# Turning half of the attention keys on VectorE: clustered attention and a gated long convolution on one Trainium2 core

## The chip, the cores and the metric

The kernel runs on one core of one Trainium2 chip. A core has five engines with a queue each: TensorE (PE in the profile, PEld for its weight loads), VectorE (DVE), ScalarE (ACT), GpSimd (POOL) and SyncE (SP), which here only issues DMA transfers. They wait for each other by semaphores. The metric is the device time of one execution in microseconds, the median of several runs.

## What is computed

Two layers follow each other. The first is attention in which a query sees only the keys of its own cluster; the cluster is the centroid with the largest cosine. The second multiplies three projections of the result, the second of them convolved over the sequence by way of a Fourier transform, and projects the product.

```python
# batch 4, heads 8, sequence 768, head size 64, 16 centroids per head
q_assign = argmax(einsum('bhsd,hcd->bhsc', q_n, c_n))      # q_n, k_n, c_n: rows of length 1
k_assign = argmax(einsum('bhsd,hcd->bhsc', k_n, c_n))
mask   = q_assign[:, :, :, None] == k_assign[:, :, None, :]
scores = where(mask, q @ k.T / 8, -1e9)
attn   = softmax(scores);  o = attn @ v
x = o.transpose(0, 2, 1, 3).reshape(B, S, 512)
x1, x2, x3 = split(x @ w_proj, 3)
x2_conv = irfft(rfft(x2, axis=1) * rfft(filter_fft, axis=0), axis=1)
out = (x1 * x2_conv * x3) @ w_out
```

The order in which the keys of a head are taken does not matter, as long as V stands in the same order.

## The kernel before

The 32 heads are worked through in eight groups `n` of four heads, and a group in two pairs `pr` of two heads. `build` makes a list of operations, each with the engines that may run it and a duration for each (`op(("PE", 1.42), ...)`), a due time, and what it reads and writes. `Plan.place` then lays them out in time: at each step the engine that can start first takes, of the operations ready for it, the one that is due first. `NUDGE` adds a number to the due time of each operation by its place in the list, `ONLY` binds some operations to one of their engines. The result is a fixed order for each engine's queue; on the chip the engines only follow it and wait for each other.

**Loads.** `load_qk` (L313 on) brings the Q and the K of a pair, two transfers each, into one of four buffers `qkraw`: partition `p` gets the rows `6p` to `6p+5` of both heads, so each transfer has 768 runs of 64 numbers (256 bytes). `load_v` (L326) brings V into one of three buffers `vraw` in one transfer, in the same row order.

**Routing** (`routing`, L572 on). Scores need Q and K with the head dimension on the partitions. For groups 2 to 7 `tr2` (L592 to L594) turns Q and K of a pair by twelve 128x128 transposes on TensorE into three PSUM banks, and three copies of 512 columns (L597) on ScalarE or VectorE bring them to `qkP`. Groups 0 and 1 do it in blocks of three transposes (`tr`, L607) with one copy of 384 columns each. Casts to bf16 (L613) make the operands `augs` of the scores. `sim` (L627) compares Q and K with the centroids; on VectorE two transposes in 32x32 blocks (L632), a maximum (L638), a comparison (L640) and one more transpose (L642, `lock=True`) give the cluster of each row; `hits` (L653, L655) and eight small transfers (`masks`, L497) add the mask rows to `augs`.

**Attention** (`attention`). For each of the six key tiles `sk` of a pair: three score blocks of 512 columns on TensorE (L84 by way of `columns`, or L82 at full width), three exponentials on ScalarE into a buffer `p` of five (L694, L697), the product with V on TensorE (`pv`, L708: eight matmuls, at least 1.29 us in the profile), and the running sum of the `p` tiles in `acc` for the softmax's denominator. The first two tiles are added in three parts on VectorE or GpSimd (L725), the others one by one on VectorE (L729). Then `acc` is summed over partitions by transfers that accumulate (L762) or by a matmul (L742), and the reciprocal goes over DRAM (L766 to L779) to `rb`, which scales the output into `xT` (L808).

**The second layer** (`hyena`) of a batch of eight heads fills the gaps of the next two groups: projections (L843 and `G`), the transform as matmuls, products on VectorE (L857 to L959), the output projection and the store. That of the last batch forms the tail.

An operation marked `lock` on GpSimd is made to wait for the last such operation of VectorE ahead of it in the plan.

Of the kernel before, what the change touches and what calls it, by code (L numbers as in the profile page):

```python
# [19 lines left out]
Alu = mybir.AluOpType  # L20
PSUM = bass.MemoryType.PSUM

B, H, S, D, NC = 4, 8, 768, 64, 16
# [9 lines left out]
NV = 3  # L33
NU = 4
ROWS = 16
LEAD = 0.0
# [228 lines left out]
def build(T):  # L265
# [27 lines left out]

    def T_(name, i):
        return lambda: getattr(T, name)[i]
# [10 lines left out]
    def alu(e):  # L306
        return T.nc.vector if e == "DVE" else T.nc.gpsimd
# [7 lines left out]
    def load_qk(n, pr, j, due, after=()):  # L315
        s = qslot[n, pr, j] = len(loads) % NQK
        loads.append(1)

        src = lambda: (T.q, T.k)[j][n // 2, 4 * (n % 2) + 2 * pr:4 * (n % 2) + 2 * pr + 2].rearrange("h (p t) d -> p t h d", t=NT)
        for x in range(2):  # L320
            for half in ((0,), (1,)) if n == pr == 0 else ((0, 1),):
                t = slice(3 * half[0], 3 * half[-1] + 3)
                op({"SP": .66, "ACT": .66} if n == 0 else ("SP", .66), lambda e, x=x, t=t: dma(e)(
                    T.qkraw[s][:, t, x], src()[:, t, x]), due, w=[("qkraw", s, x, c) for c in half],
                   byts=98e3 * len(half), kind="load", after=after, lat=.3 if n else -.5)

    def load_v(n, pr, due, after=()):
        op(("SP", .6), lambda e: T.nc.sync.dma_start(
            T.vraw[(2 * n + pr) % NV], T.v[n // 2, 4 * (n % 2) + 2 * pr:4 * (n % 2) + 2 * pr + 2].rearrange(
                "h (p t) d -> p h (t d)", t=NT)), due, w=[("vraw", (2 * n + pr) % NV)], byts=LOAD, kind="load",  # L330
           after=after)
# [242 lines left out]
    def routing(n):  # L574
# [5 lines left out]
        for u in range(8):  # L580
            z, ch = u // 2, u % 2
            pr, j = z // 2, z % 2
            due = beg + (u - (.9 * (u % 4) if n > 1 else 0)) * (end - 22 - beg) / 8 if n else 3 + u
            if n == 0 and u == 4:
                got = first_masks(0)
            s = qslot[n, pr, j]
            raw = lambda s, i: T.qkraw[s][:, i].rearrange("p h d -> p (h d)")
            if n > 1 and z % 2 == 0 and ch == 0:
                h = Bank(cls, 3)
                ss = [qslot[n, pr, x] for x in range(2)]  # L590

                def tr2(e, ss=ss, h=h):  # L592
                    for i in range(2 * NT):
                        T.nc.tensor.transpose(bank(h.ids[i // 4])[:, ts(i % 4, 128)], raw(ss[i // NT], i % NT), T.ident[:, ::-1] if 3 <= i < NT else T.ident)  # L594
                op(("PE", 1.42), tr2, due, r=[("qkraw", s, x, c) for s in ss for x in range(2) for c in range(2)] + ["ident"], w=[h], alloc=h)
                for c in range(3):
                    op(EV512, lambda e, pr=pr, c=c, h=h: copy(e, T.qkP[pr][:, ts(c, 512)], bank(h.ids[c])), due + 1.6,  # L597
                       r=[h], w=[("qkT", 2 * pr + x, y) for x, y in ((0, 0), (0, 1), (0, 2), (1, 0), (1, 1), (1, 2))[2 * c:2 * c + 2]],
                       free=[h])
            elif n < 2:  # L600
                h = Bank(cls)

                def tr(e, s=s, ch=ch, j=j, h=h):
                    if n == 0:
                        awake(h)
                    for t in range(3):
                        T.nc.tensor.transpose(ap(h)[:, ts(t, 128)], raw(s, 3 * ch + t), T.ident[:, ::-1] if ch > j else T.ident)  # L607
                op(("PE", .36 if n else .58), tr, due, r=[("qkraw", s, x, c) for x in range(2) for c in ((0, 1) if n else (ch,))] + ["ident"] + ["cold"] * (n == 0), w=[h], alloc=h)
# [22 lines left out]
        for ch in range(2):  # L631
            op(("DVE", .57), lambda e, ch=ch, h=h: V().transpose(T.sim[:, ch], bank(h.ids[ch])[:, :384]), b0 + 1.4 + .1 * ch,  # L632
               r=[h], w=[("sim", ch, 0), ("sim", ch, 1)], free=[h])
# [8 lines left out]
        op(("DVE", .98), lambda e: V().transpose(T.ohB[:], words().rearrange("p m c -> p (m c)")), b0 + 4, r=both("oh"),  # L642
           w=["ohB"], lock=True)
# [640 lines left out]
```

## Time and profile before

| | |
|---|---|
| median of three runs | 369.32 us (369.24 to 369.35) |
| profiled execution | 369.39 us |
| its span, first to last instruction | 367.7 us |
| granted clock of TensorE | 0.999 |
| transposes L594 on TensorE | 144, weight loads 15.6 us |
| copies of qkP on VectorE | 5 of 512 columns, 3.3 us; 8 of 384 columns, 4.3 us |
| DMA packets | 90,405, of which 78,248 under 512 bytes |
| transfers issued by SP | 240 |

Times in the rows of groups are: busy time in all and mean of one in ns, then the idle time of the engine just ahead of such instructions and what ended it. Matmuls overlap each other in the pipeline, so the sum of their means is more than their busy time. A line of a helper, such as L84 or L282 and L284 (`copy` on ScalarE and on the other engines), stands for all who call it; the names of the tiles tell them apart.

### The profile page before, as it was taken

To read this page: it belongs to the slowest core of one execution; us is meant where nothing else is said; L and a number is where in the kernel's file an instruction comes from. 1 tells how busy PE (TensorE), PEld (TensorE's weight loads), DVE (VectorE), ACT (ScalarE), POOL (GpSimd) and SP (SyncE) were. 2 spreads that over 40 slices of the span, in tenths; PEclk is the share of its full clock that TensorE was granted. 3 is DMA by queue.
4 is the path that set the end of the run, shared out by engine and by line. 5 is a ranking of instruction groups with operands and counts; after the bars stand their busy time and mean duration, and the time that the engine had idled before them with its cause. 6 is when DMAs were issued, how large, how long until landed. Compare 5 with 4: busy or idle time off the path is not lost.

```text
span 367.7 us, 8671 instructions
## 1 busy us (share of the span) xinstructions
PE 357.7 (97%) x3322; PEld 207.4 (56%) x3322; DVE 342.5 (93%) x479; ACT 265.0 (72%) x496; POOL 119.3 (32%) x160
## 2 busy tenths in 40 slices
PE   8899999999999999999999999999999999999985
PEld 4455554556555655655555665566554655566662
DVE  7999999997999899999999999999998999999993
ACT  7999978877986867878679756798574768434242
POOL 7734131312043824322520033351220424016610
PEclk9999999999999999999999999999999999999999
DMA  7977994555655929487658947646486650110124
GB/s 177 247 140 170 191 220 101 146 127 142 174 109 71 178 40 208 80 182 90 109 66 193 260 111 173 118 92 71 88 120 162 152 77 2 47 45 2 57 118 171
DMA packets 90405, 46.20 MB, mean 126 GB/s; under 512 B 78248, under 2 KB 84092, under 8 KB 90364
## 3 DMA queue, kind: packets, MB, share of 16 engines
q1 hardware_dynamic: 85884, 36.25, 41.0%
q0 software_dynamic: 2752, 8.98, 17.7%
q10 hardware_dynamic: 1728, 0.43, 0.5%
q8 instruction: 26, 0.43, 0.5%
q14 instruction: 15, 0.12, 0.1%
HBM read 31.59 MB, written 7.40 MB: 106 GB/s over the span
## 4 chain that ended last, share of the span: by engine, by line
PE 88%; DVE 4%; ACT 3%; issue 2%; DMA 1%; ACTq 0%; POOL 0%; DVEq 0%; POOLq 0%
PE bank L84 38%; PE pair L708 32%; PE bank L843 6%; PE bank L594 4%; PE bank L627 3%; PE bank L742 1%; PE bank L607 1%; DMA qkraw<-in_k_dram 1%; DVE acc L729 1%; PE bank L475 1%; ACT p L697 1%; DVE qkP L284 1%; ACT qkP L282 1%; ACT aug L282 0%; PE bank L799 0%
## 5 line engine op out<-in xcount | busy, mean ns | idle before, releaser
L708 PE MATMUL pair<-p,vraw 128*64 128x385 f32 x768 | 142.6, 488 | 0.0
L697 ACT ACTIVATE p<-bank 128x512 f32<-128x512 f32 x192 | 108.2, 610 | 24.1 <-PE bank L84 20.0
L729 DVE TENSOR_TENSOR acc<-p,acc 128x1536 f32<-128x1536 f32 x64 | 111.8, 1747 | 2.8 <-POOL aug L284 0.8
L84 PE MATMUL bank<-aug,aug 80*64 80x512 bf16 (+3 forms) x744 | 83.8, 326 | 1.4 <-ACT p L697 0.7
L708 PEld LDWEIGHTS pair<-p,vraw 128*64 128x64 f32 x768 | 55.4, 136 | 44.3 <-issue 37.4
L84 PEld LDWEIGHTS <-aug 80*64 80x64 bf16 (+1 forms) x744 | 45.7, 109 | 41.7 <-issue 27.1
L694 ACT ACTIVATE p<-bank 128x512 f32<-128x512 f32 x96 | 57.8, 608 | 15.2 <-PE bank L84 13.0
L762 POOL DMA_DIRECT2D acc<-acc x30 | 23.7, 801 | 84.1 <-DMA acc<-acc 34.6
L284 POOL CAST aug<-qkP 64x768 bf16<-64x768 f32 x29 | 26.8, 931 | 66.4 <-DVE acc L729 43.9
L84 PE MATMUL bank<-xT,wpj 128*64 128x384 bf16 x504 | 47.8, 326 | 0.3 <-ACT p L697 0.2
L84 PEld LDWEIGHTS <-wpj 128*64 128x64 bf16 x504 | 30.3, 110 | 14.6 <-issue 3.4
L282 ACT COPY qkP<-bank 128x512 f32<-128x512 f32 (+1 forms) x47 | 24.0, 561 | 15.0 <-PE bank L594 8.1
L725 POOL TENSOR_TENSOR acc<-p,p 128x512 f32<-128x512 f32 x16 | 21.0, 1319 | 34.9 <-DVE acc L725 18.6
L84 PEld LDWEIGHTS <-y 128*64 128x64 bf16 x472 | 23.6, 110 | 13.5 <-issue 3.4
L873 DVE TENSOR_TENSOR tm<-bank,hm 128x512 f32<-128x512 f32 x44 | 28.0, 679 | 1.4 <-PE bank L84 0.9
L84 PE MATMUL bank<-wout,y 128*64 128x512 bf16 (+1 forms) x200 | 23.6, 371 | 1.0 <-DVE y L959 1.0
L843 PE MATMUL bank<-wpj,xT 128*64 128x512 bf16 x192 | 22.8, 379 | 0.0
L282 ACT CAST aug<-qkP 64x768 bf16<-64x768 f32 x26 | 21.6, 829 | 1.5 <-DVE qkP L284 1.0
L725 DVE TENSOR_TENSOR acc<-p,p 128x512 f32<-128x512 f32 x32 | 21.1, 701 | 0.7 <-ACT x L282 0.6
L732 ACT COPY osb<-pair 128x770 f32<-128x770 f32 x16 | 13.1, 816 | 9.8 <-PE pair L708 9.8
L877 POOL TENSOR_TENSOR y<-tm 128x512 bf16<-128x512 f32 x12 | 15.2, 1278 | 13.7 <-DVE tm L873 11.6
L594 PEld LDWEIGHTS bank<-ident,qkraw 128*128 128x128 f32 x144 | 15.6, 141 | 5.8 <-ACT p L697 1.9
(176 smaller groups left out, 437.6 us busy)
## 6 DMA issues: line engine op xcount, KB each, us to landing
vraw<-in_v_dram SPq DMA_DIRECT2D x16, 384.0 KB, 5.6
qkraw<-in_q_dram SPq DMA_DIRECT2D x30, 192.0 KB, 4.1
rb<-dr SPq DMA_DIRECT2D x30, 192.0 KB, 3.4
qkraw<-in_k_dram SPq DMA_DIRECT2D x29, 192.0 KB, 3.6
out_dram<-ob SPq DMA_DIRECT2D x9, 512.0 KB, 6.7
acc<-acc POOLq DMA_DIRECT2D x10, 384.0 KB, 5.2
acc<-acc POOLq DMA_DIRECT2D x10, 192.0 KB, 4.1
y<-in_moe_filter_fft_dram SPq DMA_DIRECT2D x4, 384.0 KB
```

The costliest lines, as they stand in the source:

```text
L84: T.nc.tensor.matmul(out[64 * i:64 * i + 64], lhsT[:, 64 * i:64 * i + 64], rhs, start=start, stop=stop)
L282: T.nc.scalar.copy(out, in_)
L284: (T.nc.vector if e == "DVE" else T.nc.gpsimd).tensor_copy(out, in_)
L594: T.nc.tensor.transpose(bank(h.ids[i // 4])[:, ts(i % 4, 128)], raw(ss[i // NT], i % NT), T.ident[:, ::-1] if 3 <= i < NT else T.ident)
L694: T.nc.scalar.activation(o, ap(h).rearrange("p (a b) -> p a b", a=2), Act.Exp, scale=0.125)
L697: T.nc.scalar.activation(flat(s)[:, lo:lo + 512], ap(h), Act.Exp, scale=0.125)
L708: T.nc.tensor.matmul(o[64 * hp:64 * hp + 64, ch, :385], T.vraw[vs][:, hp, sk * D:(sk + 1) * D], T.p[slots[sk]][:, hp, 384 * ch:384 * ch + ...
L725: alu(e).tensor_tensor(o, x, y, op=Alu.add)
L729: T.nc.vector.tensor_tensor(T.acc[os], T.p[slots[sk]][:, :, :S], T.acc[os], op=Alu.add)
L762: op(("POOL", .8), lambda e, rows=rows: T.nc.gpsimd.dma_start(flat_()[:rows], flat_()[rows:2 * rows], accum_op=Alu.add), te, r=[], w=AK, b ...
L843: T.nc.tensor.matmul(ap(h)[64 * i:64 * i + 64], T.xT[xs][:, kt, c:c + 64], T.wpj[:, kt, DM:2 * DM], start=kt == 0, stop=kt == ND - 1)
L873: op(("DVE", .68), lambda e, i=i, cs=cs, r=r, h=h: T.nc.vector.tensor_tensor(T.tm[r][:, cs], ap(h), hmrow(i, (0, 2, 2, 3)[2 * r + cs]), op ...
```

## The change

- `TURN` names the twelve pairs of groups 2 to 7. Their K is no longer turned by TensorE. One VectorE transpose in 32x32 blocks takes `qkraw` (128x768, f32) straight to the K half of `qkP`, with no PSUM bank and no copy.
- For that, K is loaded in another layout: each head in two halves of the head dimension, four transfers of 32 partitions and 768 runs of 32 numbers (128 bytes). A partition holds 24 rows' halves.
- The keys then stand in another order, and V of these pairs is loaded to match it, in four transfers of 32 partitions.
- Q of these pairs is turned as in groups 0 and 1: two blocks of three transposes with a copy of 384 columns each.
- The first two key tiles are added in one instruction of 128x1536 on VectorE or GpSimd.
- The transpose at L642 loses its `lock`, and loads of groups 2 to 7 are planned with a later landing (`lat=.8`).
- `NUDGE` and `ONLY` are replaced as a whole, so that the order on every queue is another. In it, among other things, five copies of `ob` and four scalings of tables go from VectorE to ScalarE, four additions into `y` from VectorE to GpSimd, and 31 of the 372 pairs of half-width score matmuls of 512 or 256 columns become full-width ones.

```diff
+TURN = [(n, pr) for n in range(2, NG) for pr in range(2)]
...
-NUDGE = {0:1.857,1:2.33,2:2.705,
+NUDGE = {0:-130.596,1:-5378.268,2:-8.351,
...
     load_qk:
-        for x in range(2):
+        turned = j == 1 and (n, pr) in TURN
+        for x in range(2) if turned else ():
+            for y in range(2):
+                op(("SP", .6), lambda e, x=x, y=y: dma(e)(
+                    T.qkraw[s][64 * x + 32 * y:64 * x + 32 * y + 32].rearrange("p t h d -> p (t h d)").rearrange("p (c d) -> p c d", d=32),
+                    T.k[n // 2, 4 * (n % 2) + 2 * pr + x].rearrange("(p c) d -> p c d", c=4 * NT)[:, :, 32 * y:32 * y + 32]), due,
+                   w=[("qkraw", s, x, y)], byts=130e3, kind="load", after=after, lat=.8)
+        for x in range(2) if not turned else ():
...
-                   byts=98e3 * len(half), kind="load", after=after, lat=.3 if n else -.5)
+                   byts=98e3 * len(half), kind="load", after=after, lat=.8 if n > 1 else .3 if n else -.5)
     load_v:
+        for x in range(4) if (n, pr) in TURN else ():
+            op(("SP", .6), lambda e, x=x: T.nc.sync.dma_start(
+                T.vraw[(2 * n + pr) % NV][32 * x:32 * x + 32], T.v[n // 2, 4 * (n % 2) + 2 * pr:4 * (n % 2) + 2 * pr + 2].rearrange(
+                    "h (i p t) d -> p i h (t d)", p=4, t=NT)[x]), due, w=[("vraw", (2 * n + pr) % NV, x)], byts=LOAD / 4, kind="load",
+               after=after, lat=.8)
...
     routing:
-            if n > 1 and z % 2 == 0 and ch == 0:
+            if (n, pr) in TURN and j:
+                if ch == 0:
+                    op(("DVE", .96), lambda e, s=s, z=z: V().transpose(
+                        T.qkP[z // 2][:, ts(1, S)], T.qkraw[s][:].rearrange("p t h d -> p (t h d)").rearrange("p (q t d) -> p t q d", q=4, d=32)),
+                       due, r=[("qkraw", s, h_, y) for h_ in range(2) for y in range(2)], w=qk(z, 0) + qk(z, 1))
+            elif n > 1 and (n, pr) not in TURN and z % 2 == 0 and ch == 0:
...
-            elif n < 2:
+            elif n < 2 or (n, pr) in TURN:
...
-           w=["ohB"], lock=True)
+           w=["ohB"], lock=False)
...
     attention:
-            op(("PE", 1.3), pv, due, r=[("p", slots[sk], u) for u in range(3)] + [("vraw", vs), "eps"] +
+            op(("PE", 1.3), pv, due, r=[("p", slots[sk], u) for u in range(3)] + [("vraw", vs, x) for x in range(4)] + ["eps"] +
...
-                for u in range(3):
-                    def part(e, u=u):
...
-                        alu(e).tensor_tensor(o, x, y, op=Alu.add)
-                    op({"DVE": .63, "POOL": 1.5}, part, due - 1 + .2 * u, r=[("p", slots[i], u) for i in range(2)], w=[("acc", os, u)], lock=True)
+                def part(e):
+                    alu(e).tensor_tensor(T.acc[os], T.p[slots[0]][:, :, :S], T.p[slots[1]][:, :, :S], op=Alu.add)
+                op({"DVE": 1.75, "POOL": 3.5}, part, due - 1, r=PK(0) + PK(1), w=AK, lock=True)
```

More of the change, by code (lines that the diff above doesn't have):

```diff
@@ L324, in load_qk @@
                     T.qkraw[s][:, t, x], src()[:, t, x]), due, w=[("qkraw", s, x, c) for c in half],
-                   byts=98e3 * len(half), kind="load", after=after, lat=.3 if n else -.5)
+                   byts=98e3 * len(half), kind="load", after=after, lat=.8 if n > 1 else .3 if n else -.5)
     def load_v(n, pr, due, after=()):
+        for x in range(4) if (n, pr) in TURN else ():
[3 more added lines that the diff above has]
+               after=after, lat=.8)
+        if (n, pr) in TURN:
+            return
         op(("SP", .6), lambda e: T.nc.sync.dma_start(
             T.vraw[(2 * n + pr) % NV], T.v[n // 2, 4 * (n % 2) + 2 * pr:4 * (n % 2) + 2 * pr + 2].rearrange(
-                "h (p t) d -> p h (t d)", t=NT)), due, w=[("vraw", (2 * n + pr) % NV)], byts=LOAD, kind="load",
-           after=after)
+                "h (p t) d -> p h (t d)", t=NT)), due, w=[("vraw", (2 * n + pr) % NV, x) for x in range(4)], byts=LOAD, kind="load",
+           after=after, lat=.8 if n > 1 else 0.0)
     def centroids():
@@ L607, in tr @@
                         T.nc.tensor.transpose(ap(h)[:, ts(t, 128)], raw(s, 3 * ch + t), T.ident[:, ::-1] if ch > j else T.ident)
-                op(("PE", .36 if n else .58), tr, due, r=[("qkraw", s, x, c) for x in range(2) for c in ((0, 1) if n else (ch,))] + ["ident"] + ["cold"] * (n == 0), w=[h], alloc=h)
+                op(("PE", .58 if n == 0 else .36), tr, due, r=[("qkraw", s, x, c) for x in range(2) for c in ((0, 1) if n else (ch,))] + ["ident"] + ["cold"] * (n == 0), w=[h], alloc=h)
                 op(EV384 if n != 1 else {"ACT": .48}, lambda e, z=z, ch=ch, h=h: copy(e, T.qkT[z][:, ch], ap(h)[:, :384]),
```

11 lines of the change are left out of this document (2 added, 9 removed).

## The prediction

> **What bounds the kernel now.** I read the busy shares first, then the chain of waits, the groups by form, the busy time in stretches of 12 us, and the waits of the queues.
>
> ```profile
> span 367.7 us, 8671 instructions
> PE 357.7 (97%) x3322; PEld 207.4 (56%) x3322; DVE 342.5 (93%) x479; ACT 265.0 (72%) x496; POOL 119.3 (32%) x160
> ...
> PE 88%; DVE 4%; ACT 3%; issue 2%; DMA 1%; ACTq 0%; POOL 0%; DVEq 0%; POOLq 0%
> PE bank L84 38%; PE pair L708 32%; PE bank L843 6%; PE bank L594 4%; PE bank L627 3%; PE bank L742 1%; PE bank L607 1%; DMA qkraw<-in_k_dram 1%; DVE acc L729 1%; PE bank L475 1%; ACT p L697 1%; DVE qkP L284 1%; ACT qkP L282 1%; ACT aug L282 0%; PE bank L799 0%
> ```
>
> TensorE is idle for only 10.0 us of the span and makes up 88% of the chain that ended last. The transposes of line 594, which the change halves, are 4.4% of that chain, 16.2 us. VectorE is a close second, idle for 25.2 us.
>
> The windows (columns: window, its length, then busy us and count of PE, PEld, DVE, ACT and POOL, granted clock, DMA share, GB/s):
>
> ```profile
> 132.00:144.00 12.00, 12.00 (x114) 6.55 (x112) 11.73 (x15) 9.73 (x18) 1.98 (x3) 1.00 0.63 121
> 276.00:288.00 12.00, 12.00 (x114) 6.30 (x112) 10.30 (x13) 5.83 (x12) 1.51 (x2) 1.00 0.74 204
> 336.00:348.00 12.00, 12.00 (x134) 7.67 (x132) 11.86 (x21) 3.40 (x7) 6.02 (x6) 1.00 0.11 45
> ```
>
> TensorE is full in the attention part and in the tail, at full clock; VectorE has 0.1 to 1.7 us free in each of these 12. So work taken from TensorE shortens the run only if VectorE, which takes over part of it, does not get longer itself.
>
> **The change part by part.** The prices, by form:
>
> ```profile
> L729 DVE TENSOR_TENSOR acc<-p,acc 128x1536 f32<-128x1536 f32 x64 | 111.8, 1747 | 2.8 <-POOL aug L284 0.8
> ...
> L725 DVE TENSOR_TENSOR acc<-p,p 128x512 f32<-128x512 f32 x32 | 21.1, 701 | 0.7 <-ACT x L282 0.6
> L725 POOL TENSOR_TENSOR acc<-p,p 128x512 f32<-128x512 f32 x16 | 21.0, 1319 | 34.9 <-DVE acc L725 18.6 <-ACT p L694 6.6 <-DVE dn L775 4.5
> L594 PE MATMUL bank<-ident,qkraw 128*128 128x128 f32 x144 | 18.4, 277 | 0.0
> ...
> L282 ACT COPY qkP<-bank 128x512 f32<-128x512 f32 x31 | 17.0, 597 | 8.6 <-PE bank L594 8.1 <-DVE dn L772 0.3
> ...
> L632 DVE STREAM_TRANSPOSE sim<-bank 128x384 f32<-128x384 f32 x14 | 7.4, 559 | 0.7 <-PE bank L627 0.7
> L642 DVE STREAM_TRANSPOSE ohB<-oh 128x768 bf16<-128x768 bf16 x7 | 6.8, 978 | 0.2
> ```
>
> *TensorE.* Groups 2 to 7 have 12 head pairs, each with 12 transposes; 144 become 72. By busy time the 72 are worth 18.4/2 = 9.2 us, by their share of the chain 16.2/2 = 8.1 us. One block of 12 takes 1.47 us in the chain, so half of twelve blocks is 8.8 us. I take the middle of the bounds, 8.6. In the instruction lists of the two builds the other matmuls are the same work (some scores as one full-width matmul in place of two halves). The switches between widths rise from 59 to 61; a matmul block behind a transpose takes 1.45 us for 1.29, so two more cost 0.3. Net: -8.3 us.
>
> *VectorE.* Added: 12 transposes of 128x768 f32. No row has f32 from SBUF. Lower bound: the 384-wide f32 row has 0.559 us, and twice the elements cost at least that. Upper: two of it, 1.12. The bf16 row of just this size says 0.978, and I take it: 12 x 0.98 = +11.7 (6.7 to 13.4). The page "VectorE: DVE Perf Modes" of the Trainium skill, section "The three transpose paths", gives 311 ns for 128x128 bf16 on VectorE; six of these, as an estimate, would be 1.87 us a tile and +22.4 in all, 10.7 more than by row L642, whose 0.978 us for those six blocks disagrees with it.
>
> The first addition: of 48 thirds, 32 ran here (-21.1) and 16 on GpSimd; now 10 whole ones run here (10 x 1.747 = +17.5) and 6 on GpSimd. The rest comes out of the lists with row means: evictions of qkP 5 of 512 out, 5 of 384 in (-3.3 +2.8), aug casts +4 (+2.4), ob copies -5 (-3.4), four table scalings to ScalarE (-3.0), four y additions to GpSimd (-2.7), and some fifteen single instructions of 0.5 to 1.0 us, net -6.4. Sum: +11.7 - 21.1 + 17.5 - 0.5 + 2.4 - 3.4 - 3.0 - 2.7 - 6.4 = -5.5, so 337.0 us (332 to 338.7). On a span near 359 that is 94%, the share it has now.
>
> *ScalarE.* 31 evictions of 512 out (-17.0), 19 of 384 in (+8.3, from 7.0 us for 16), five ob copies, four scalings and some copies in: +1.9, 267 us of 359. It has the room; zero on the path.
>
> *GpSimd.* Six whole additions at three times 1.319 are 23.7, against 21.0; casts -2.8, y and yy work +9.1, two memsets -1.5: +7.5, 127 us. Zero on the path while it is under 40% busy; but each of the six now holds a buffer for 4.0 us instead of 1.3, and the next accumulation on VectorE waits behind it. If that cover went, six waits of 2.6 us are 16 us.
>
> *DMA and SP.* K tiles come in quarters of 32 partitions, 128-byte runs, V tiles in quarters.
>
> ```profile
> q1 hardware_dynamic: 85884, 36.25, 41.0%
> ...
> qkraw<-in_k_dram SPq DMA_DIRECT2D x29, 192.0 KB, 3.6
> ...
> SPq L776 <- DVE dn L775: 49.5, 11, 10.2
> SPq L1005 <- ACT ob L282: 36.0, 4, 19.6
> SPq L323 <- PE bank L594: 18.4, 5, 11.2
> ```
>
> The SP queue issues 299 transfers for 240; one issue takes 0.62 us in the median, so +37 us on a queue that stands in three waits alone for 104 us (the last block: who waited for whom, total, times, longest). What is queued behind a K quarter that waits for its buffer are the mask rows (L497), the denominator chain (L766 to L779) and output. I take zero, because in the lists at least four accumulations (L729) stand between the transpose that frees a K buffer and the next one on that buffer. A group has eight, and in the chain the eight groups share the stretch from 23 to 321 us, 37 us each: a lead of some 18 us, while a load needs 3.6 after its issue and four issues 2.5. Packets: 24 issues of 768 runs become 48 of 768, +18,432. The queue's mean is 41.0% x 16 x 367.7 us / 85,884 = 28.1 ns, so +32 us of all 16 engines, 9 points more on about 60%. Bounds: zero, or the 2.7 us that one tile's extra 1536 packets take, on every tile: 32 us. TensorE's product with V now waits for four V quarters instead of one; everything on TensorE stands behind it, but V too is a buffer of three ahead. Removing the port lock of the transpose at L642 and the longer planned landing of loads shift order only.
>
> *New order.* The due times are replaced wholly, so the idle time can go either way. By row durations the lists leave about the same TensorE work (40 us) behind the last product with V, and sim, mask and score blocks follow each other as before. I leave TensorE's idle 10.0 us as it is.
>
> **Sum.** The profiled execution took 369.39 us, 1.7 outside its span, and lies 0.07 above the median 369.32. 369.39 - 8.6 + 0.3 = **361.1 us**. As said, 0.2% (0.7 us) is what a measurement of this kernel can tell from no change.
>
> **Rivals.**
> *VectorE becomes the bound.* For: it is idle least after TensorE, and its in-order queue carries the accumulation that frees p. Against: its share stays. If its idle 25.2 us is what its dependences cost, the span is 337.0 + 25.2 = 362.2 and the time 363.9; with the transposes at 1.12 it is 365.6.
>
> *The order also closes gaps.* For: the block of twelve needed three PSUM banks at once, two blocks of three need one each. If half of TensorE's idle goes, 369.39 - 8.3 - 5.0 = 356.1.
>
> *Late K (slower).* Place: the transpose on VectorE, which waits for four quarters in an in-order queue; behind it stand accumulations and evictions, and behind those TensorE. For: DMA is 0.7 to 1.0 busy in several windows, and the loads double their packets. Against: no transpose waited for a load after the start, and the lead above. Price: 2.7 us for each late tile; from the fourth late tile (10.8) it outweighs 8.3. With six late: 361.1 + 16 = 377. The Trainium skill, "DMA: Bandwidth & Descriptors", "Rules for kernel authors", speaks for it: coalesce small transfers, and do not split one over partition ranges. No run here shows the split yet.
>
> *The transposes cost double on VectorE (slower).* At 1.87 us each VectorE has 347.7, with its idle 372.9, time 374.6. The page named above would give this; the row L642 speaks against it.
>
> *Nothing is freed.* If matmuls shown as busy only wait inside, the time stays at 369.4. Against: blocks of one kind repeat to 0.02 us (1.29 for L708).
>
> **Chances.** Forecast 0.53 (359 to 363.5), VectorE bound 0.17, closed gaps 0.11, nothing freed 0.04, late K 0.11, double transposes 0.04. Faster by over 0.2%: 0.53 + 0.17 + 0.11 = 0.81; within: 0.04; slower: 0.15. The range runs from 356, the closed gaps, to 369.6, and leaves the slower cases and part of the gaps out, 0.19. The likeliest case alone is 359 to 363.5.
>
> **What would show it.** Right: 72 transposes of 128x128 fewer on TensorE, its busy time near 349 with about 10 us idle; 12 stream transposes of qkP near 0.98 us that wait for nothing; VectorE near 337. Wrong: VectorE waiting for qkraw loads (late K), transposes near 1.9, TensorE idle well over 10 us with VectorE full, or ScalarE held by p buffers behind the six long additions on GpSimd.

## The result and the profile after

The changed kernel takes 372.79 us (median, 370.94 to 373.36) against 369.56 us for the kernel before, measured beside it: ratio 1.0078, 95% interval 1.0055 to 1.01. The forecast was 361.1. The profiled execution took 372.84 us. Executions over 1.5% above the fastest of the same kernel are left out of all ratios: four of a_three's six (379.3 to 380.7 us), one each of a_noturn_old and a_vtwo_dd, and one of the kernel before. Line numbers are those of the changed kernel (before + 1 in the helpers, + 12 to 20 behind the loads: L84 is L85 now, L725 is L737, L729 is L741, L766 is L778).

The page of the changed kernel, shares first, then the chain of waits by engine and by line:

```profile
span 371.1 us, 8436 instructions
PE 354.5 (96%) x3191; PEld 202.5 (55%) x3191; DVE 337.6 (91%) x449; ACT 264.3 (71%) x502; POOL 121.5 (33%) x152
...
PE 56%; DVE 21%; ACT 6%; DMA 6%; issue 5%; POOL 2%; SPq 2%; DVEq 0%; ACTq 0%; POOLq 0%
```

VectorE is busy almost to the microsecond as forecast (337.6 for 337.0), and still the run is longer. TensorE's share of the chain fell from 88% to 56%; VectorE's rose from 4% to 21%, that of transfers from 1% to 6%. TensorE's busy time fell by 3.2 us only, and its idle time rose from 10.0 to 16.6. The busy time of matmuls contains some waiting: at 85.41 us a group of 16 similarity products (L647) took 2.51 us, where five other such groups of this kernel took 1.50; a weight load inside it waited 0.72 us for the turn on VectorE (L605).

The groups that answer to the priced ones:

```profile
L741 DVE TENSOR_TENSOR acc<-p,acc 128x1536 f32<-128x1536 f32 x64 | 111.9, 1749 | 4.3 <-POOL acc L737 1.6
...
L737 POOL TENSOR_TENSOR acc<-p,p 128x1536 f32<-128x1536 f32 x6 | 20.7, 3458 | 8.7 <-DVE uv L874 4.4 <-ACT p L714 2.8 <-DMA dd<-acc 1.4
L627 PE MATMUL bank<-ident,qkraw 128*128 128x128 f32 x120 | 18.6, 281 | 0.8 <-DMA qkraw<-in_k_dram 0.8
L737 DVE TENSOR_TENSOR acc<-p,p 128x1536 f32<-128x1536 f32 x10 | 17.7, 1765 | 2.9 <-ACT p L714 1.4 <-ACT p L717 1.4
L605 DVE STREAM_TRANSPOSE qkP<-qkraw 128x768 f32<-128x768 f32 x12 | 11.5, 961 | 1.4 <-DMA qkraw<-in_k_dram 1.4
```

Unit prices were about right: a turn takes 0.961 us (0.978 taken), a whole addition on GpSimd 3.46 (4.0), and the transposes of TensorE went from 18.4 + 7.2 = 25.6 us to 18.6, 7.0 less (8.6 taken).

The windows of before, and one more (240:252, where before had TensorE busy for 11.23 of 12; columns as in the prediction):

```profile
132.00:144.00 12.00, 11.25 (x100) 5.95 (x98) 10.67 (x13) 8.82 (x16) 4.92 (x5) 1.00 0.48 94
240.00:252.00 12.00, 7.99 (x100) 5.86 (x98) 11.12 (x16) 6.16 (x12) 4.17 (x4) 1.00 0.61 129
276.00:288.00 12.00, 12.00 (x104) 7.28 (x102) 10.51 (x12) 5.81 (x11) 1.95 (x2) 1.00 0.63 157
```

At full clock TensorE now stops in places. The chain of waits of the changed kernel says for what (start, length, what; all in us), ahead of 132:144 and inside 240:252:

```profile
124.11 0.64 SPq L324
...
124.92 5.10 DMA dd<-acc
...
130.16 3.46 POOL acc L737
133.62 0.02 issue
133.64 0.60 ACT p L717
...
241.75 2.12 DMA vraw<-in_v_dram
243.88 0.47 ACT ohT L673
...
246.29 5.25 DMA aug<-ohT
251.54 0.04 issue
251.58 3.68 PE bank L85 x50
```

First place: K quarters (L324) stand on SP ahead of the denominators' first transfer; a first addition on GpSimd wants the same buffer `acc`, waits for that transfer, then runs 3.46 us while the exponential behind it (L717) waits for a score buffer that it holds; TensorE is idle for 0.68 us behind that. Second place: the mask rows. TensorE, ScalarE (`ohT`, L673) and SP take turns, each waiting for the one before: TensorE is idle for 0.83, 1.08 and 1.08 us until ScalarE is done and for 1.01 us until the mask transfers land, the 4.0 us that are missing in this window. The chain names a V quarter ahead of `ohT`, but `ohT` reads no V, the four V quarters were issued by 242.66, and SP then waited from 243.60 to 245.29 until `ohT` was written. So the quarters did not hold up these masks, and a_noturn_old below, with the old loads, has the same three waits for ScalarE (0.83, 1.08, 1.08, from 238.8 us on): this place belongs to the new order. A chain shows one way to the end; what the parts cost is measured below.

### The profile page after: what moved, and what is told of

Its sections match the earlier page's. It is cut to its first block, busy times and chain, and to the rows that moved or that the text cites. A ratio compares the mean times of both kernels' runs of the same rounds, so it can differ in the third digit from the quotient of the medians.

```text
span 371.1 us, 8436 instructions
## 1 busy us (share of the span) xinstructions
PE 354.5 (96%) x3191; PEld 202.5 (55%) x3191; DVE 337.6 (91%) x449; ACT 264.3 (71%) x502; POOL 121.5 (33%) x152
## 3 DMA queue, kind: packets, MB, share of 16 engines
q1 hardware_dynamic: 105772, 36.05, 43.1%
## 4 chain that ended last, share of the span: by engine, by line
PE 56%; DVE 21%; ACT 6%; DMA 6%; issue 5%; POOL 2%; SPq 2%; DVEq 0%; ACTq 0%; POOLq 0%
PE bank L85 23%; PE pair L728 23%; DVE acc L741 5%; DMA qkraw<-in_k_dram 2%; PE bank L855 2%; DVE xT L820 2%; PE bank L83 2%; PE bank L627 2%; PE bank L647 2%; DVE sd L956 2%; DVE tm L869 1%; DMA aug<-ohT 1%; DVE acc L737 1%; DMA dd<-acc 1%; DVE yy L966 1%
## 5 line engine op out<-in xcount | busy, mean ns | idle before, releaser
L717 ACT ACTIVATE p<-bank 128x512 f32<-128x512 f32 x192 | 109.1, 612 | 19.0 <-PE bank L85 10.7
L741 DVE TENSOR_TENSOR acc<-p,acc 128x1536 f32<-128x1536 f32 x64 | 111.9, 1749 | 4.3 <-POOL acc L737 1.6
L85 PE MATMUL bank<-aug,aug 80*64 80x256 bf16 (+3 forms) x682 | 75.5, 327 | 4.2 <-DMA aug<-ohT 1.4
L85 PEld LDWEIGHTS <-aug 80*64 80x64 bf16 (+1 forms) x682 | 42.4, 109 | 41.4 <-issue 29.6
L85 PE MATMUL bank<-xT,wpj 128*64 128x384 bf16 x488 | 44.8, 326 | 1.2 <-ACT ohT L673 1.1
L285 POOL CAST aug<-qkP 64x768 bf16<-64x768 f32 x26 | 21.3, 823 | 66.1 <-DVE acc L741 23.3
L85 PEld LDWEIGHTS <-wpj 128*64 128x64 bf16 x488 | 30.3, 110 | 13.3 <-issue 4.3
L85 PEld LDWEIGHTS <-y 128*64 128x64 bf16 x456 | 23.9, 110 | 14.6 <-issue 5.1
L85 PE MATMUL bank<-wout,y 128*64 128x512 bf16 (+1 forms) x200 | 24.2, 372 | 1.3 <-DVE y L971 0.9
L889 POOL TENSOR_TENSOR y<-tm 128x512 bf16<-128x512 f32 x16 | 20.2, 1274 | 14.0 <-DVE tm L885 7.7
L737 POOL TENSOR_TENSOR acc<-p,p 128x1536 f32<-128x1536 f32 x6 | 20.7, 3458 | 8.7 <-DVE uv L874 4.4
L283 ACT COPY qkP<-bank 128x384 f32<-128x384 f32 x35 | 15.8, 480 | 10.0 <-PE bank L85 4.6
L283 ACT COPY ob<-bank 128x512 f32<-128x512 f32 x22 | 12.4, 594 | 13.4 <-PE bank L85 9.9
L737 DVE TENSOR_TENSOR acc<-p,p 128x1536 f32<-128x1536 f32 x10 | 17.7, 1765 | 2.9 <-ACT p L714 1.4
L627 PE MATMUL bank<-ident,qkraw 128*128 128x128 f32 x120 | 18.6, 281 | 0.8 <-DMA qkraw<-in_k_dram 0.8
```

What stands on the lines that cost most here:

```text
L85: T.nc.tensor.matmul(out[64 * i:64 * i + 64], lhsT[:, 64 * i:64 * i + 64], rhs, start=start, stop=stop)
L283: T.nc.scalar.copy(out, in_)
L285: (T.nc.vector if e == "DVE" else T.nc.gpsimd).tensor_copy(out, in_)
L717: T.nc.scalar.activation(flat(s)[:, lo:lo + 512], ap(h), Act.Exp, scale=0.125)
L737: alu(e).tensor_tensor(T.acc[os], T.p[slots[0]][:, :, :S], T.p[slots[1]][:, :, :S], op=Alu.add)
L741: T.nc.vector.tensor_tensor(T.acc[os], T.p[slots[sk]][:, :, :S], T.acc[os], op=Alu.add)
```

## The experiments

Two families. Names with b_ keep the order of the kernel before, instruction for instruction, and edit what single operations issue; names with a_ keep the order of the changed kernel. All times are medians; "against before" is the difference to the median of the kernel before measured beside it (369.39 to 369.94 us).

### The parts of the change in the old order

**b_noK**, the transposes and nothing in their place:

```diff
-    for i in range(2 * NT):
-        T.nc.tensor.transpose(bank(h.ids[i // 4])[:, ts(i % 4, 128)], raw(ss[i // NT], i % NT), ...)
+    for i in range(NT):
+        T.nc.tensor.transpose(bank(h.ids[i // 3])[:, ts(i % 3, 128)], raw(ss[0], i), ...)
...
-    op(EV512, lambda e, ...: copy(e, T.qkP[pr][:, ts(c, 512)], bank(h.ids[c])), due + 1.6,
+    op(EV512, lambda e, ...: copy(e, T.qkP[pr][:, ts(c, 384)], bank(h.ids[c])[:, :384]) if c < 2 else None, due + 1.6,
```

> The kernel before, in its own order, with the 72 transposes of the keys of groups 2 to 7 and the copies that they fed simply left out (the keys stay what group 1 left; no turn on VectorE, the old loads, first additions in three parts): the output is not the reference's. It shows what the TensorE work that the change removes is worth in the old order when nothing is put in its place. If TensorE alone bounds the kernel, as the prediction has it: 361 to 363 us, the 7 us of PE rows come off in full. If the kernel is bound by TensorE and VectorE together: 364 to 368 us, since part of the 7 us turns into TensorE waiting for VectorE.

365.44 us, ratio 0.9883 (0.9859 to 0.9908): 4.2 us less. Its page:

```profile
PE 351.5 (97%) x3250; PEld 200.5 (55%) x3250; DVE 341.5 (94%) x477; ACT 257.9 (71%) x486; POOL 121.0 (33%) x160
...
PE 73%; DVE 16%; issue 3%; DMA 3%; ACT 2%; POOL 1%; SPq 0%; DVEq 0%; POOLq 0%
```

With 7 us of TensorE and some copies gone, VectorE, whose busy time barely moved (342.5 to 341.5), takes 16% of the chain for 4%. The starts of the products with V show it place by place: against the kernel before they come 0.66 us earlier at most of the twelve pairs, and fall back by 0.3 to 1.0 us at five places. At five places TensorE now waits more than 0.2 us for VectorE, 2.8 us in all, where the kernel before doesn't wait; three of the waits (0.74, 0.25 and 0.92 us) are for the last step of the routing on VectorE, L642:

```profile
148.07 0.35 PE L84 MATMUL bank<-ohB,tri 128*64 128x384 bf16 x2 [0.74 <-DVE ohB L642]
...
234.55 0.52 PE L84 MATMUL bank<-ohB,tri 128*64 128x384 bf16 x4 [0.92 <-DVE ohB L642]
```

So this is the most that the freed transposes are worth in the old order: about half of the 8.3 us forecast, with nothing added anywhere.

**b_turn_old**, the same with the turn on VectorE at the place of the transposes, old loads:

```diff
     def tr2(e, ss=ss, h=h, pr=pr):
...
+        V().transpose(T.qkP[pr][:, ts(1, S)],
+            T.qkraw[ss[1]][:].rearrange("p t h d -> p (t h d)").rearrange("p (q t d) -> p t q d", q=4, d=32))
```

> b_turn2 with the loads of the kernel before (two transfers for a K tile, one for V of a pair): the turn on VectorE alone, in the old order; the keys stand in the wrong places, so the output is not the reference's. b_noK took 365.4 us and b_turn2 378.4. If the 60 more issues on SP's queue (b_turn2's denominators wait 6.3 us behind a row of such issues) are what the turn costs: 366 to 369 us. If VectorE's 11.5 us are: 375 to 378 us.

373.08 us, ratio 1.0095 (1.0082 to 1.0108). Twelve turns of 0.96 us, 11.5 us of VectorE, cost 7.8 us over b_noK (+3.6 against before, from -4.2). The page:

```profile
PE 353.9 (95%) x3250; PEld 202.1 (54%) x3250; DVE 350.6 (95%) x489; ACT 258.4 (70%) x486; POOL 120.6 (33%) x160
...
PE 45%; DVE 38%; issue 8%; ACT 3%; DMA 3%; POOL 1%; SPq 0%; DVEq 0%; ACTq 0%; POOLq 0%
```

VectorE and TensorE now share the chain. TensorE's idle time rose from 12.1 us in b_noK to 17.0 (span less busy time), and three of its longest waits are again for the routing's last step (`ohB`: 0.93, 0.89 and 1.82 us). Neither of the two outcomes foreseen came in full: the value lies between them, on the side of VectorE.

**b_turn2**, with the quarter loads of K and V as well:

```diff
+    def quarters(n, pr, s, x):
+        for y in range(2):
+            T.nc.sync.dma_start(T.qkraw[s][64 * x + 32 * y:64 * x + 32 * y + 32]..., T.k[...][:, :, 32 * y:32 * y + 32])
...
-        op(("SP", .6), lambda e: T.nc.sync.dma_start(T.vraw[...], ...
+        op(("SP", .6), vq if n > 1 else lambda e: T.nc.sync.dma_start(T.vraw[...], ...     # vq: four quarters
```

> As b_turn, with the turn on VectorE put where TensorE's transposes stood, ahead of the loads that use the same buffers again (in b_turn it stood behind some of them, and read the next keys): the turn and the new loads in the old order, first additions in three parts. If the new order costs the time: 363 to 366 us. If the turn, the loads or VectorE's added 11.5 us do: 370 to 376 us; the difference to b_noK is then the price of the turn with its loads.

378.41 us, ratio 1.0232 (1.0197 to 1.0268): the loads cost another 5.1 us (+8.7 against before, from +3.6). Where they cost can be read off. SP's queue in b_turn2 (start, length in all, line, transfer, how many):

```profile
156.16 3.75 SPq L508 DMA_DIRECT2D aug<-ohT  x5
160.00 1.54 SPq L329 DMA_DIRECT2D qkraw<-in_k_dram  x2
161.58 1.35 SPq L508 DMA_DIRECT2D aug<-ohT  x2
163.03 1.17 SPq L792 DMA_DIRECT2D rb<-dr  x2
164.25 1.30 SPq L329 DMA_DIRECT2D qkraw<-in_k_dram  x2
165.59 0.64 SPq L508 DMA_DIRECT2D aug<-ohT  x1
166.33 1.93 SPq L336 DMA_DIRECT2D vraw<-in_v_dram  x4
168.45 1.04 SPq L779 DMA_DIRECT2D dd<-acc  x1
```

and the chain of b_turn2 behind it:

```profile
168.45 6.27 DMA dd<-acc
...
174.83 1.91 DVE acc L738 x3
```

From the first mask row to dd<-acc the queue takes 12.3 us; the same piece in the kernel before took 8.6 (152.54 to 161.10). The last accumulation ahead of dd<-acc was issued at 159.62 and such a transfer lands after 3.8 us here (median), so the denominators lay ready for some 5 us; in the kernel before (issued at 155.61, 3.5 us to land) it was some 2. The transfer itself took longer too: 6.27 us, where in the kernel before the next transfer, which waits for it, went out 4.5 us behind it (161.10 to 165.58); why isn't shown. These 3.0 and 1.8 us are most of the 5.6 by which the products with V fall further behind b_turn_old's at this place. A first addition (L738) on VectorE waits 5.1 us for `acc`, and with it the whole of its in-order queue; TensorE was busy for 19.64 us of the 24 from 168 to 192, and its granted clock there was 0.86, so part of the loss is a slower TensorE. The execution profiled is the longest of the six (380.48 us, mean granted clock 0.988); those at 0.993 or more took 376.9 to 377.6 us, about 4 us over b_turn_old. Each issue is only 0.6 us; what counts is how many stand ahead of one that something waits for.

**b_whole2**, one whole first addition in place of three parts:

```diff
+    left.append(u)
+    if len(left) == {3: 3, 9: 1}.get(2 * n + pr, 2):
+        alu(e).tensor_tensor(T.acc[os], T.p[slots[0]][:, :, :S], T.p[slots[1]][:, :, :S], op=Alu.add)
-    ...
-    alu(e).tensor_tensor(o, x, y, op=Alu.add)
```

> As b_whole, with each whole addition put at the second of the three places (the third for one tile, the first for another), where its two key tiles are both written and not yet overwritten: in b_whole two of them stood behind the exponentials that overwrite their input. 5 of the 16 are on GpSimd. If the whole addition costs the time: 372 us or more, with the 3.5 us addition on GpSimd on the chain of waits. If not: 368.5 to 370.5 us.

373.96 us, ratio 1.0111 (1.0087 to 1.0135): 4.3 us more, though the rows of the additions on VectorE went from 21.1 to 19.2 us. The profile shows two things that can be the reason. One is the exponentials. Rows of the kernel before (L697, L694: idle time ahead of them and what ended it), then of b_whole2, where the addition is L721:

```profile
L697 ACT ACTIVATE p<-bank 128x512 f32<-128x512 f32 x192 | 108.2, 610 | 24.1 <-PE bank L84 20.0 <-PE pair L708 2.1 <-DVE acc L725 0.6
L694 ACT ACTIVATE p<-bank 128x512 f32<-128x512 f32 x96 | 57.8, 608 | 15.2 <-PE bank L84 13.0 <-DVE acc L725 1.2 <-POOL acc L725 0.6
```

```profile
L697 ACT ACTIVATE p<-bank 128x512 f32<-128x512 f32 x192 | 108.2, 609 | 26.5 <-PE bank L84 19.9 <-DVE acc L725 2.3 <-POOL acc L721 1.6
L694 ACT ACTIVATE p<-bank 128x512 f32<-128x512 f32 x96 | 57.8, 607 | 15.6 <-PE bank L84 12.2 <-DVE acc L721 2.9
```

In the kernel before they wait 2.4 us for accumulations (0.6 + 1.2 + 0.6), here 6.8 (2.3 + 1.6 + 2.9). Three parts give a score buffer back third by third; the whole addition starts when all thirds are there and holds both buffers to its end.

The other is on VectorE, which is busy for 346.2 us, 3.7 more than before. Four of its instructions that overlap a whole addition on GpSimd took 1.92, 2.50, 1.12 and 2.40 us, where the median of their kind is 0.17, 0.56, 0.68 and 0.68, and each ended 0.4 to 1.0 us behind that addition. Two of the four (timeline):

```profile
144.48 3.75 POOL L721 TENSOR_TENSOR acc<-p,p 128x1536 f32<-128x1536 f32 x1
147.30 1.92 DVE L769 TENSOR_SCALAR dn<-dn 128x12 f32<-128x12 f32 x1
...
186.03 3.45 POOL L721 TENSOR_TENSOR acc<-p,p 128x1536 f32<-128x1536 f32 x1 [0.99 <-DVE ohB L642]
187.41 2.50 DVE L950 TENSOR_TENSOR yy<-sd 128x384 f32<-128x384 f32 x1
```

In the kernel before, one instruction beside an addition on GpSimd is as long (L640, 2.03 us for 0.96); in the changed kernel there is one of 1.14 us for 0.69. How the 4.3 us divide between the buffers and the held instructions was not measured.

**b_both2**, both edits together:

> b_turn2 and b_whole2 together: everything of the change but its new order. If the new order costs the time: 364 to 368 us, well under the changed kernel's 372.8. If the new order is what keeps the loss small: above 373 us, the sum of what the two parts cost alone.

384.02 us, ratio 1.036 (1.0319 to 1.0402): 14.4 us more than before, 5.6 more than b_turn2. This is the change without its new order (but with the lock at L642, and with five whole additions on GpSimd for six), and the changed kernel is 11 us faster than this. So the new order is the part that pays. One thing that it does better can be seen: here four VectorE instructions are held by GpSimd's additions, as in b_whole2, there one. How much of the 11 us that is, no run shows.

Two earlier forms were misplaced. **b_turn** put the turn where the last copy stood, **b_whole** the addition at the last of three places:

> The order of the kernel before, instruction for instruction, with the keys of groups 2 to 7 loaded in 128-byte runs and turned by VectorE, V in their order, and the first additions still in three parts. If the loads cost the time (four issues and 3,072 packets for a K tile, four issues for V): 370 to 374 us, with DMA qkraw or vraw, or SP's queue, on the chain of waits for 10 us or more. If the new order costs it: 363 to 367 us, since the 7 us of TensorE's transposes go and nothing else moves. If the whole first addition costs it: 363 to 367 us as well.

> The kernel before, instruction for instruction, with one change: the third of the three parts of each first addition becomes the whole addition (10 on VectorE, 6 on GpSimd), the first two go. If the whole addition costs the time: 372 to 375 us, with an acc line on GpSimd on the chain. If the loads or the new order cost it: 369 to 370.5 us, no change that can be told.

381.77 and 378.14 us. In b_turn the turns stood behind the next loads of their buffers and waited for those; in b_whole two additions stood behind exponentials that overwrite their input. These times say nothing of the change.

### What holds the changed kernel in its own order

**a_oldloads** edits the loads alone (V likewise in one transfer, as in the kernel before):

```diff
-    T.qkraw[s][64 * x + 32 * y:64 * x + 32 * y + 32]..., T.k[...].rearrange("(p c) d -> p c d", c=4 * NT)[:, :, 32 * y:32 * y + 32]), due,
+    T.qkraw[s][:, :, x], src()[:, :, x]) if y == 0 else None, due,
```

> The changed kernel with its order, its turn on VectorE and its whole additions, but the keys loaded as in the kernel before (two transfers of 256-byte runs for a tile) and V in one transfer for a pair of heads: 59 issues fewer on SP. The keys then stand in the wrong places, so the output is not the reference's. If the loads cost the time: 363 to 367 us. If the new order or the whole addition costs it: 371 to 374 us.

370.82 us, ratio 1.004 (1.0016 to 1.0064), twelve runs from 368.91 to 374.16: the loads cost about 1.8 us here, not the 5.1 of the old order. The interval touches that of the changed kernel, so 1.8 is at the edge of what can be told.

**a_k256** edits the length of the runs of K:

```diff
-    T.k[...].rearrange("(p c) d -> p c d", c=4 * NT)[:, :, 32 * y:32 * y + 32]), due,
+    T.k[...].rearrange("(c p) d -> p c d", p=32)[:, 12 * y:12 * y + 12]), due,
```

> The changed kernel with one thing different: each K quarter is read in 12 runs of 256 bytes for a partition and not in 24 of 128, as many bytes and as many issues, half the packets; the keys stand in the wrong places, so the output is not the reference's. If the small packets cost the time: as low as with the old loads, 363 to 367 us. If the number of issues on SP does: 371 to 373 us, while the old loads bring it down. If neither does: 371 to 373 us, as the old loads.

371.56 us, ratio 1.0059 (1.0046 to 1.0071): 1.1 us less than the changed kernel, within the intervals. Half the packets are no large part of it. The page of the changed kernel agrees; its hardware queue moved 23% more packets than before in 2 points more of the time:

```profile
q1 hardware_dynamic: 105772, 36.05, 43.1%
```

**a_noturn**, the turns left out:

```diff
-    op(("DVE", .96), lambda e, s=s, z=z: V().transpose(T.qkP[z // 2][:, ts(1, S)], ...),
+    op(("DVE", .96), lambda e: None,
```

> The changed kernel with the 12 turns on VectorE left out (the loads stay, the keys stay what group 1 left, so the output is not the reference's). If VectorE's busy time is what bounds the new order beside TensorE: 362 to 367 us, most of the 11.5 us back. If the loads and SP's queue are: 369 to 372 us.

372.21 us, ratio 1.0063 (1.0043 to 1.0083): VectorE loses 11.5 us of work and the run some 0.5, less than can be told. The new order has the turns where little waits for them (in the changed kernel ScalarE 2.9 us, TensorE's weight loads 0.7). In the chain of a_noturn TensorE has 72% and VectorE 10%, and dd<-acc, aug<-ohT and rb<-dr are still on it, with 5.9, 4.7 and 6.3 us.

**a_noturn_old**, turns and new loads both out:

> The changed kernel with the turns on VectorE left out and the old loads as well (a_noturn and a_oldloads together; the output is not the reference's). If VectorE's turn and the loads stand in for one another as the last to end: 361 to 365 us, far more than the sum of the two alone. If the rest (the order, the whole additions) holds the kernel: 369 to 370.5 us, the sum of 0.6 and 2.0.

369.04 us, ratio 0.9987 (0.9969 to 1.0005): 3.8 us less than the changed kernel. The sum of the two alone is 2.3 (0.5 and 1.8), so they stand in for one another a little. With the turns out, the loads are worth 3.3 us, clear of the intervals. In the profiles a_noturn falls behind a_noturn_old at two places, by 1.6 us behind the dd<-acc at 122.77 and by 2.6 behind the rb<-dr at 199.23; both belong to the denominators. With the turn and its loads gone, and TensorE's 7 us gone too, the new order only reaches the kernel before.

**a_firstdve** moves the six additions of GpSimd to VectorE, at the same places:

```diff
+        if o.fn.__name__ == "part":
+            o.on = "DVE"
...
-    alu(e).tensor_tensor(T.acc[os], T.p[slots[0]][:, :, :S], T.p[slots[1]][:, :, :S], op=Alu.add)
+    T.nc.vector.tensor_tensor(T.acc[os], T.p[slots[0]][:, :, :S], T.p[slots[1]][:, :, :S], op=Alu.add)
```

> The changed kernel with its six first additions on GpSimd (3.46 us each) put on VectorE at the same places (1.77 us each, 10.6 us more on VectorE); the output is the reference's. If the whole additions on GpSimd cost the time: 367 to 370 us. If VectorE's time does: 375 us or more. If neither: 372 to 374 us.

381.07 us, ratio 1.0304 (1.027 to 1.0337): 10.6 us more on VectorE cost 8.2, nearly what the turn cost in the old order. VectorE bounds this kernel where work is put on it that the order wasn't made for, though 11.5 us taken off it elsewhere gave back nothing.

**a_three** and **a_nopool** look at the additions themselves:

> The changed kernel with each first addition in three parts again, one behind the other at the place and on the engine of the whole one, so that a part can start when its own exponential is done; the output is the reference's. If the whole addition costs the time by waiting for all three exponentials: 369 to 371 us. If only the longer busy time counts (three parts take 2.1 us on VectorE for 1.77, 3.9 on GpSimd for 3.46): 373 to 376 us.

```diff
-    alu(e).tensor_tensor(T.acc[os], T.p[slots[0]][:, :, :S], T.p[slots[1]][:, :, :S], op=Alu.add)
+    for u in range(3):
+        ...
+        alu(e).tensor_tensor(o, x, y, op=Alu.add)
```

372.7 and 373.5 us, ratio 1.0094 (1.0077 to 1.0112), from two executions only. It shows that parts at the place of the whole gain nothing, and no more than that.

> The changed kernel with five of its six first additions on GpSimd left out (those of groups 1 to 7; the denominators are wrong, so the output is not the reference's): 17.3 us of GpSimd and the wait of what uses the two score buffers again. If these additions hold the new order: 365 to 369 us. If not: 371.5 to 373.5 us.

```diff
+    if e != "POOL" or n == 0:
         alu(e).tensor_tensor(T.acc[os], T.p[slots[0]][:, :, :S], T.p[slots[1]][:, :, :S], op=Alu.add)
```

372.44 us, ratio 1.009 (1.0059 to 1.0122): no gain that can be told. The addition of 3.46 us stood on the chain of waits, and leaving it out hardly moved the end: being on the chain isn't a price.

**a_ddpool** takes dd<-acc off SP:

```diff
-    op(("SP", .6), lambda e: T.nc.sync.dma_start(T.dd[os], flat_()[:ROWS]), te + 2, r=AK,
+    op(("SP", .6), lambda e: T.nc.gpsimd.dma_start(T.dd[os], flat_()[:ROWS]), te + 2, r=AK,
```

> The changed kernel with one thing different: the 10 transfers dd<-acc are issued by GpSimd, behind its own accumulations, and not by SP; the output is the reference's. If SP's queue ahead of them costs the time: 369 to 371.5 us. If it does not, or GpSimd's queue is no better: 372 to 374 us; above 375 us if GpSimd's own work is now behind them.

373.91 us, ratio 1.0119 (1.0094 to 1.0143), no gain. It doesn't settle what SP's queue costs: the transfer of the first place went out at 124.8 us, where SP had issued it at 124.92, so GpSimd's queue was as late.

**a_few, b_turn_few and a_vtwo_dd** were to save issues on SP with the same bytes (both halves of a head's keys in one transfer; V one transfer a head):

```diff
-    T.qkraw[s][64 * x + 32 * y:...]..., T.k[...].rearrange("(p c) d -> p c d", c=4 * NT)[:, :, 32 * y:32 * y + 32]), due,
+    T.qkraw[s][64 * x:64 * x + 64]..., T.k[...].rearrange("(p c) (y d) -> y p c d", c=4 * NT, d=32)) if y == 0 else None, due,
...
-    T.vraw[...][32 * x:32 * x + 32], T.v[...].rearrange("h (i p t) d -> p i h (t d)", p=4, t=NT)[x]), due,
+    T.vraw[...][:, x], T.v[... + x].rearrange("(i p t) d -> p i (t d)", p=4, t=NT)) if x < 2 else None, due,
```

> The changed kernel with the same two forms of load: 48 issues fewer on SP, everything else as it is, the output is the reference's. The old loads gave 370.8 us, with twice as long runs. If the number of issues is what counts: 370 to 371.5 us. If the packets are: 372 to 373.5 us.

> b_turn2 with the same bytes in the same 128-byte runs, but one issue for both 32-column halves of a head (two for a K tile) and two for V: 48 issues fewer on SP, the output is the reference's. If the number of issues on SP is what costs: within 2 us of b_turn_old. If the packets are: near b_turn2's 378.4 us.

> The changed kernel with V in two transfers a pair of heads, one for each head, and not in four (24 issues fewer on SP), and with the first transfer of the denominators (dd<-acc) issued by GpSimd behind its own accumulations and not by SP; the output is the reference's. If SP's queue is what holds the denominators, and the additions that use the buffer again: 368 to 371 us. If not: 372 to 374 us.

(a_vtwo_dd has the second of these edits and that of a_ddpool.) 531.27, 538.73 and 392.39 us: all of them far out of what was expected. In a_few 25 of SP's 249 issues took more than 6 us, up to 11.4, and the mean granted clock of the execution profiled was 0.87. Two of them, each behind a merged K issue:

```profile
91.02 0.58 SPq L324 DMA_DIRECT2D qkraw<-in_k_dram  x1
91.65 8.91 SPq L331 DMA_DIRECT2D qkraw<-in_q_dram  x1
...
101.34 0.52 SPq L324 DMA_DIRECT2D qkraw<-in_k_dram  x1
101.96 7.05 SPq L331 DMA_DIRECT2D qkraw<-in_q_dram  x1
```

In a_vtwo_dd, whose K is in quarters, the longest issue of a K quarter took 7.2 us for 3.6 in the changed kernel. The trace doesn't show which DMA engines a transfer used. The page "DMA: Bandwidth & Descriptors" of the Trainium skill, section "Why a DMA increments its semaphore by 16 and not by 1", says that a transfer runs on the largest number of engines up to 16 that divides the slowest dimension of both sides; that dimension is 2 in the merged K and 4 in the merged V. As an estimate by it, 1,536 packets at the 24 ns mean of the changed kernel (43.1% x 16 x 371.1 us / 105,772) are 18 us on two engines and 2.3 on sixteen, which would go with the long issues; no run here tells it from another cause. So the issue count was not tested by itself; the old loads, with fewer issues and another layout, stay the measure of what the loads cost.

## Why the prediction was wrong

In the old order the change adds up like this, all against the kernel before: transposes off -4.2, turn on VectorE +7.8, its loads +5.1, whole additions +5.6 on top (+4.3 alone), together +14.4; the new order -11.1; result +3.2. The prediction had -8.3, 0, 0, 0 and 0. The -11.1 is what remains of the sum: no run has the new order with the old work. In the new order the same parts cost less (turn 0.5, loads 1.8, both 3.8).

- **What bounds the kernel.** "TensorE ... makes up 88% of the chain that ended last" was read as one bound, and the 8.3 us were passed to the end in full. That step failed first: b_noK shows 4.2 at most, with nothing put on VectorE. VectorE, idle for only 25.2 us, ends nearly as late as TensorE at some places, with the routing's last step above all: b_noK's TensorE waits for it there, and b_turn_old's longer. The chain names one of two that end together. The prediction's own warning that work moved to VectorE must not lengthen it was the right thought, but it was checked with a sum over the run.
- **The size of the term.** By their rows the transposes gave 7.0 us for 8.6 taken, under the lower bound of 8.1; by the 0.66 us at a pair in b_noK, twelve pairs are 7.9. This was the smaller fault.
- **VectorE -5.5, so 337.0.** The sum was right (337.6), the conclusion not. The turn's 11.5 us cost 7.8 in the old order, and the additions, whose rows on VectorE got shorter (forecast 21.1 to 17.5, in b_whole2 21.1 to 19.2), cost 4.3. Busy time summed over the run doesn't say what stands behind each microsecond of it.
- **GpSimd zero on the path "while it is under 40% busy".** Wrong as a rule, since it depends on the order. In the old one b_whole2 lost 4.3 us at 31% busy, where 16 were given as the price without cover. The wait that the prediction named, a buffer held longer, is there: the exponentials waited 5.2 us for VectorE's accumulations and whole additions (2.3 + 2.9) and 1.6 for GpSimd's. The prediction didn't think of the VectorE instructions that are held meanwhile. In the new order zero nearly held: a_nopool gave back 0.7 us, less than can be told. Its busy time was 121.5 us for the 127 forecast.
- **SP and the loads zero.** The lead of four accumulations was argued for the K tile, and there it nearly held: the twelve turns waited 1.4 us in all. (One transfer of K, at 43.91 us, is on the chain for 8.66; with the old loads it is there too, at 42.39 for 9.29.) What was late was what stood behind the quarters on SP, the denominators, which the prediction listed and did not price: 5.1 us in the old order, in the new one 1.8 with the turns and 3.3 without. That the quarters hold up mask rows, no run here shows.
- **The new order "as it is".** It was the largest term, -11.1 us as the remainder of the sum, and the only good one beside the transposes.
- **The rivals.** VectorE becomes the bound came nearest in kind (b_turn_old: 38% of the chain), but was priced with VectorE's idle time held at 25.2 us; it was 33.5. Late K had the right resource and the wrong waiter: six turns waiting 2.7 us each did not happen, queue places ahead of dd<-acc did. The page "DMA: Bandwidth & Descriptors" of the Trainium skill, section "Rules for kernel authors", asks not to split a transfer over partition ranges; b_turn2 against b_turn_old goes the same way by 5.1 us (with runs of half the length for K in the same edit), while the merged transfers of a_few were far worse. Double-cost transposes fell: 0.961 us, where the page "VectorE: DVE Perf Modes" of the Trainium skill, section "The three transpose paths", gave an estimated 1.87. Closed gaps did not come true: TensorE's idle time rose from 10.0 to 16.6 us, and what the new order saves it saves on the parts that the change adds.

Open: why the new order, with turns and new loads out (a_noturn_old), is 3.6 us slower than b_noK, which has as little work for TensorE. Of the 3.8 us between the spans of the two profiles, 2.7 are TensorE's busy time (354.2 for 351.5 us) and 1.1 its idle time; the three waits for ScalarE at the mask rows, 3.0 us, are in a_noturn_old and not in b_noK. Besides the order itself, the whole additions on VectorE are the difference that was not taken out by itself in the new order; a_nopool speaks against the five on GpSimd. The parts' prices in the old order also contain that this order was made for other work. No version here beat the kernel before with the reference's output.

## What to carry to other kernels

Where two engines are busy over 90%, leave the work out first and add nothing: that run (here -4.2 us) is the ceiling of any move between them in that order, and here it was less than the work's own time. Price work moved to the second engine by what stands behind it in its queue (in the old order 0.7 us of run for each us of VectorE), a larger operation by the buffers that it holds and by what the other engine gets done beside it, and more transfers by what waits for the queue behind them, not by the queue's mean occupancy. Ask of a change that comes with a new order what its parts do in the old one; the order can hide most of a loss.

## What the hardware showed unasked

With two 32-partition transfers of K merged into one of 64 partitions, in the same 128-byte runs, and with V in two transfers for four, 25 issues of SP took 6 to 11.4 us for about 0.6, and the kernel 158 us longer (531.27 for 372.79). What fills up was not tried. In b_whole2, VectorE instructions of 0.17 to 0.68 us (the medians of their kinds) took 1.12 to 2.50 us where they overlapped a 128x1536 addition on GpSimd, and ended 0.4 to 1.0 us behind it.
